# Windowed attention and a two-layer network in one program: values' parts side by side as one stationary block, and float32 transposes without copies

## The chip, the cores and the metric

The program runs on one core of a Trainium2 chip. Its time is device microseconds of one execution; three runs of the kernel before took 1107.52, 1108.76 and 1111.5 us (median 1108.76). One further look at it is a profiled execution, from which all rows below come. "Span" is the time from its first to its last instruction.

The core has a matrix engine (TensorE, PE in the profile, with its loads of stationary blocks shown as PEld), three engines for elementwise work (VectorE or DVE, ScalarE or ACT, GpSimd or POOL) and a queue that starts transfers (SP). Each takes its instructions in the order in which they stand.

## The reference

Two parts follow each other. The first is attention over 8 batches and 8 heads of 64 columns with 512 local and 32 global positions: global queries see everything, local queries see the 32 global keys and the local keys at most 32 away.

```python
s_g = scale * np.matmul(q_g, k_all.transpose(0, 1, 3, 2))
out_g = np.matmul(sm(s_g), v_all)
s_ll = scale * np.matmul(q_l, k_l.transpose(0, 1, 3, 2))
mask = np.abs(pos[:, None] - pos[None, :]) <= window
s_ll = np.where(mask, s_ll, -1000000000.0)
s_lg = scale * np.matmul(q_l, k_g.transpose(0, 1, 3, 2))
a_l = sm(np.concatenate([s_lg, s_ll], axis=-1))
out_l = np.matmul(a_l, np.concatenate([v_g, v_l], axis=2))
```

Its 8 x 544 rows of 512 columns (4352 rows) go through two layers, with weights of 512 x 2048 and 2048 x 512 that arrive as float64:

```python
h = x @ w_in
g = h * (1.0 / (1.0 + np.exp(-h)))
return (g @ w_out).astype(np.float32)
```

## The kernel before

**Parts.** To get more than the precision of the type float32r, each operand of a matmul is split into an upper part (a cast to float32r on ACT) and a lower part (the value less its upper part, on DVE or POOL). A product is three matmuls: upper by upper, upper by lower, lower by upper.

**Local attention** goes in 128 steps, 16 for a batch: a chunk c of 128 queries (4 of them) for a pair of heads (4 of them). A step has these pieces, each a function whose name begins with `st_`: load queries and keys; split them; scores on TensorE, then mask, exponential and division on DVE and ACT, into one of two buffers `probs` (lines 369 to 382); a transfer that copies `probs` into the float32r tile `rr` (line 385), since an engine that writes float32r would round; load the values, split them into `vhi` and `vlo` (lines 350 to 353); the turn: four transposes by the identity on TensorE (line 393), whose result is split into `pt_hi` on ACT and `pt_lo` on DVE (lines 396 to 398), while POOL puts beside each 32 columns of probabilities of the global queries (lines 404 to 406); and the product with the values (line 421). For each of the two heads that is three terms by two tiles of keys, with a stationary block of 128 x 64 values and 160 or 128 moving columns; in the last chunk all twelve have 160. ACT and DVE then split the product (64 rows for each head) into `xh` and `xl`, the input of the layers (lines 427 and 428), and DVE adds the 32 columns of the global queries up in `acc` (lines 433 and 435).

**Global attention** has its own pieces, named `g_`. `g_move` copies the probabilities by two transfers into float32r tiles, `g_turn` transposes them (lines 310 and 313).

**The layers** run over blocks of three or two tiles of 128 rows. A block has 16 rounds. The first layer of a round is 12 matmuls (line 550) and takes the four slices of `xh` and `xl` in turn, so the slice of the last pair of heads stands in its last three; the second layer is three matmuls for each tile (lines 569 to 571). The attention for the next block stands between them: every piece has a due time, counted in steps (`DUE`), and `fill` issues the pieces that are due after every few matmuls. The last piece of a block is therefore near its next block's start. The first block's attention stands alone at the beginning, together with the conversion of the weights, 2.6 us of DVE work for half a slice (lines 233 to 236).

TensorE's instructions stand as the program issues them. On the other engines a scheduler places them. The buffers `pt_hi` and `pt_lo` exist once, `probs` and the products' splits twice; in the banks of TensorE's results each of scores, transposes and products has one once the layers run.

Of the kernel before, what the change touches and what calls it, by code (L numbers as in the profile page):

```python
# [33 lines left out]
NEG = -8.0e9              # times the scale of 1/8: -1e9  # L34
SCALE = 0.125

# [1 line left out]
SIZES = [3, 2] + [3] * 9 + [2]       # token tiles in each block of the two layers  # L38
NLATE = 4                            # slices of the weights that take the place of the first buffers
# [19 lines left out]
PRE, PACE, LOOK = 0, 0.75, 1         # weights converted during the first steps  # L59
END = 0.6                            # how far the attention is ahead of a block  # L60
# [22 lines left out]
BUFS = dict(qk=[2, 2], raw=2, rr=1, p=2, vraw=2)  # L83
# [7 lines left out]
ND = 28  # L91

@with_exitstack
def attention_moe_kernel(ctx: ExitStack, tc: tile.TileContext, qk0_in, qk_in, v_in, gqk, wts, out):
# [7 lines left out]
    # buffers of the first steps, in two parts that later hold the last slices of the weights  # L102
# [6 lines left out]
    # until the layers start, attention has their banks too  # L109
# [33 lines left out]
    # probabilities: columns past the window stay zero  # L143
    probs = []
    for i in range(BUFS["p"]):
        t = const.tile([P, 2, 2 * P], F32, name=f"probs{i}")
        nc.gpsimd.memset(t, 0.0)
        probs.append(t)
# [239 lines left out]
    def st_turn(k, b, c, pr):  # L388
# [3 lines left out]
        for i in range(4):  # L392
            nc.tensor.transpose(t[:, i * P : (i + 1) * P].bitcast(F32R), rr[:, i * P : (i + 1) * P], ident)  # L393
# [274 lines left out]
```

## Time and profile before

| | |
|---|---|
| runs, median of three | 1108.76 us (1107.52 to 1111.5) |
| profiled execution: span | 1108.1 us |
| TensorE busy | 1042.5 us, mean granted clock 0.972 |
| DVE busy | 798.5 us |
| ACT busy | 725.1 us |
| POOL busy | 228.5 us |
| SP: copies of probabilities for local steps | 128 of 256 KB |

The profiled execution's own time beside its span is not listed; the span is 0.7 us below the median of the runs and inside their range. A row of a timeline gives start and duration in us, the engine, the line, the operation, `result<-operands`, and the shape (for a matmul stationary block, then moving columns). Matmuls overlap: the spacing of their starts says what one costs. A row of a grouped view ends with busy us and mean ns of one, then the engine's idle time just before and what ended it.

### The profile page before, as it was taken

Reading aid. Unit: us, or ns where it says so; the run is one execution under the profiler, and the core shown is the slowest. Engines: PE = TensorE matmul, PEld = TensorE weight load, DVE = VectorE, ACT = ScalarE, POOL = GpSimd, SP = SyncE. Lnnn points to the kernel's source line nnn. Section 1 sums busy time; section 2 is a strip of 40 time slices with the busy share of each in tenths; the row PEclk is TensorE's granted clock in tenths of the full one; section 3 lists DMA queues with packets and bytes.
Section 4 is the critical chain, followed back from the end, with each engine's and each line's share of the span. In section 5 each row is a group of like instructions: output and inputs, shape, how many; then the busy total and the mean of one; then the engine's idle time right before and its main releaser. Section 6 shows DMA issues by size and latency. Waiting matters only on the chain.

```text
span 1108.1 us, 21579 instructions
## 1 busy us (share of the span) xinstructions
PE 1042.5 (94%) x6824; PEld 947.8 (86%) x6824; DVE 798.5 (72%) x2467; ACT 725.1 (65%) x1933; POOL 228.5 (21%) x441
## 2 busy tenths in 40 slices
PE   5647889999999999999999999999999999999998
PEld 4646778898999999999989999999999999889996
DVE  6989998777778867766667877777777768863322
ACT  7876676776677766766567776667666658763232
POOL 8756775321100111001010111101100011100000
PEclk8678899999999999999999999999999999999999
DMA  8576554543343443342233443334333324420000
GB/s 249 179 219 188 182 170 130 156 121 117 109 145 115 138 138 110 113 148 83 82 112 112 147 130 117 111 116 158 109 109 120 111 92 148 138 76 20 1 30 19
DMA packets 74800, 134.76 MB, mean 122 GB/s; under 512 B 10432, under 2 KB 30400, under 8 KB 74688
## 3 DMA queue, kind: packets, MB, share of 16 engines
q1 hardware_dynamic: 74688, 133.40, 38.8%
q8 instruction: 54, 0.88, 0.3%
q14 instruction: 58, 0.48, 0.1%
HBM read 86.44 MB, written 8.91 MB: 86 GB/s over the span
## 4 chain that ended last, share of the span: by engine, by line
PE 80%; DVE 10%; DMA 3%; issue 3%; ACT 3%; POOL 1%; SPq 0%; DVEq 0%; ACTq 0%; POOLq 0%
PE h L550 31%; PE out L569 11%; PE out L571 10%; PE out L570 10%; PE o L421 8%; PE s L369 4%; PE t L393 3%; DVE w L234 2%; DVE w L236 1%; DMA rr<-probs 1%; DMA raw_w<-in_wts_dram 1%; DVE raw_w L233 1%; DVE pt_lo L397 1%; ACT probs L377 1%; DVE probs L373 1%
## 5 line engine op out<-in xcount | busy, mean ns | idle before, releaser
L550 PE MATMUL h<-xh,w_hi 128*128 128x384 f32 (+1 forms) x768 | 255.6, 333 | 0.1
L550 PE MATMUL h<-xh,w_lo 128*128 128x384 f32 (+1 forms) x768 | 252.3, 329 | 0.0
L550 PE MATMUL h<-xl,w_hi 128*128 128x384 f32 (+1 forms) x768 | 252.1, 328 | 0.0
L569 PE MATMUL out<-w_hi,gh 128*128 128x512 f32 x544 | 224.8, 413 | 0.0
L571 PE MATMUL out<-w_hi,gl 128*128 128x512 f32 x544 | 215.6, 396 | 3.0 <-DVE gl L560 1.8
L570 PE MATMUL out<-w_lo,gh 128*128 128x512 f32 x544 | 214.7, 395 | 0.0
L556 ACT ACTIVATE t<-h 128x384 f32<-128x384 f32 (+1 forms) x192 | 90.5, 471 | 186.2 <-PE h L550 175.8
L404 POOL CAST pt_hi<-pgt 128x64 fp32r<-128x64 f32 (+1 forms) x160 | 50.4, 327 | 726.1 <-PE o L421 719.2
L557 DVE SCALAR_TENSOR_TENSOR t<-t,h 128x384 f32<-128x384 f32 (+1 forms) x192 | 101.6, 529 | 122.7 <-ACT t L556 121.7
L550 PEld LDWEIGHTS h<-xh,w_hi 128*128 128x128 f32 x768 | 145.4, 189 | 6.0 <-ACT xh L427 0.6
L550 PEld LDWEIGHTS h<-xl,w_hi 128*128 128x128 f32 x768 | 145.5, 189 | 5.4
L550 PEld LDWEIGHTS h<-xh,w_lo 128*128 128x128 f32 x768 | 145.3, 189 | 0.0
L560 DVE TENSOR_TENSOR gl<-t,gh 128x384 fp32r<-128x384 f32 (+1 forms) x192 | 107.3, 559 | 48.5 <-PE out L571 43.1
L571 PEld LDWEIGHTS out<-w_hi,gl 128*128 128x128 f32 x544 | 102.8, 189 | 28.4 <-DVE gl L560 4.6
L377 ACT ACTIVATE probs<-probs,st 128x224 f32<-128x224 f32 x256 | 121.4, 475 | 7.3 <-DVE st L373 6.2
L373 DVE CUSTOM_DVE_ANT_0 probs<-s,mask 128x224 f32<-128x224 f32 x256 | 89.3, 384 | 50.4 <-PE s L369 47.0
L421 PE MATMUL o<-pt_hi,vhi 128*64 128x160 f32 (+1 forms) x512 | 99.4, 238 | 20.1 <-ACT pt_hi L396 7.8
L570 PEld LDWEIGHTS out<-w_lo,gh 128*128 128x128 f32 x544 | 103.6, 190 | 11.2
L569 PEld LDWEIGHTS out<-w_hi,gh 128*128 128x128 f32 x544 | 103.2, 190 | 11.4 <-ACT gh L559 0.4
L559 ACT CAST gh<-t 128x384 fp32r<-128x384 f32 (+1 forms) x192 | 94.6, 493 | 21.2 <-DVE t L557 17.8
L421 PE MATMUL o<-pt_hi,vlo 128*64 128x160 f32 (+1 forms) x512 | 96.3, 237 | 0.0
L421 PE MATMUL o<-pt_lo,vhi 128*64 128x160 f32 (+1 forms) x512 | 79.8, 238 | 16.3 <-DVE pt_lo L397 11.8
(82 smaller groups left out, 2016.5 us busy)
## 6 DMA issues: line engine op xcount, KB each, us to landing
raw<-in_qk_dram SPq DMA_DIRECT2D x100, 352.0 KB, 3.0
rr<-probs SPq DMA_DIRECT2D x128, 256.0 KB, 2.3
vraw<-in_v_dram SPq DMA_DIRECT2D x128, 128.0 KB, 2.4
raw_w<-in_wts_dram SPq DMA_DIRECT2D x28, 512.0 KB, 4.0
raw_g<-in_gqk_dram SPq DMA_DIRECT2D x32, 304.0 KB, 2.8
out_dram<-o SPq DMA_DIRECT2D x32, 256.0 KB, 2.6
raw<-in_qk_dram SPq DMA_DIRECT2D x28, 240.0 KB, 3.6
rg<-pg SPq DMA_DIRECT2D x16, 256.0 KB, 2.4
```

The costliest lines, as they stand in the source:

```text
L373: nc.vector.tensor_tensor_reduce(out=p[:, u, :W], in0=s[:, u * W : (u + 1) * W], in1=mask_of[c], scale=-SCALE, scalar=3.0e38, op0=ALU.add, ...
L377: nc.scalar.activation(p[:, u, :W], p[:, u, :W], AF.Exp, bias=st[:, u : u + 1], scale=-1.0, accum_out=st[:, 2 + u : 3 + u])
L404: nc.gpsimd.tensor_copy(out=pt_hi[:n, :, a, P:], in_=g)
L421: nc.tensor.matmul(o[:D, u * wide : u * wide + m], v[:, a, u, :], pt[:, u, a, :m], start=(i == 0), stop=(i == len(terms) - 1))
L550: nc.tensor.matmul(h[:, :nt], wt, x[:, c, :nt], start=(i == 0), stop=(i == 3 * NCC - 1))
L556: nc.scalar.activation(t[:, :nt], h[:, :nt], AF.Tanh, scale=0.5)
L557: nc.vector.scalar_tensor_tensor(out=t[:, :nt], in0=t[:, :nt], scalar=1.0, in1=h[:, :nt], op0=ALU.add, op1=ALU.mult)
L559: nc.scalar.copy(out=gh[:, :nt], in_=t[:, :nt])
L560: nc.vector.tensor_tensor(out=gl[:, :nt], in0=t[:, :nt], in1=gh[:, :nt].bitcast(F32), op=ALU.subtract)
L569: nc.tensor.matmul(o, gh[:, sl], wh, start=(f == 0), stop=False)
L570: nc.tensor.matmul(o, gh[:, sl], wl, start=False, stop=False)
L571: nc.tensor.matmul(o, gl[:, sl], wh, start=False, stop=(f == NF - 1))
```

## The change

1. **Values.** `vhi` and `vlo` become halves of one tile `vv`: for a key tile and head 64 upper columns, then 64 lower ones. The upper part of the probabilities is multiplied with all 128 columns at once, so its products with upper and lower values come out on rows 0 to 63 and 64 to 127. The lower part of the probabilities still meets the upper values alone. Four matmuls for a head instead of six.
2. **Halves.** ACT copies the lower 64 rows from TensorE's result to a new tile `xs`, DVE adds the upper 64 rows to it; so for both heads. Then ACT casts `xs` into `xh` for both heads at once (128 rows), and DVE (steps 0 to 23) or POOL (from 24, `POOLX`) subtracts it for `xl`. The sum of the global queries' columns moves from DVE to POOL, 128 rows at once.
3. **Transposes.** `probs` is the operand itself, as float32, with a float32 identity; the copies to `rr` are gone, and those of `g_move` too. In the first 12 steps there are five buffers `probs` instead of two. The check that `pg` is free waits for `g_turn`.

On TensorE, the product of step 91, the last of a block (`o91` is the result; the number after a tile's name is the step). Before:

```order
L421 MATMUL o91_9862<-pt_hi0_126,vhi91_9748 64x160
L421 MATMUL o91_9862<-pt_hi0_126,vlo91_9749 64x160
L421 MATMUL o91_9862<-pt_hi0_126,vhi91_9748 64x128
L421 MATMUL o91_9862<-pt_hi0_126,vlo91_9749 64x128
L421 MATMUL o91_9862<-pt_lo0_127,vhi91_9748 64x160
L421 MATMUL o91_9862<-pt_lo0_127,vhi91_9748 64x128
```

These six are one head's; six like them follow. With the change:

```order
L413 MATMUL o91_9358<-pt_hi0_130,vv91_9249 128x160
L415 MATMUL o91_9358<-pt_lo0_131,vv91_9249 64x160
L413 MATMUL o91_9358<-pt_hi0_130,vv91_9249 128x128
L415 MATMUL o91_9358<-pt_lo0_131,vv91_9249 64x128
L413 MATMUL o91_9358<-pt_hi0_130,vv91_9249 128x160
L415 MATMUL o91_9358<-pt_lo0_131,vv91_9249 64x160
L413 MATMUL o91_9358<-pt_hi0_130,vv91_9249 128x128
L415 MATMUL o91_9358<-pt_lo0_131,vv91_9249 64x128
```

That is both heads, in the same place between the layers' matmuls; wide and narrow ones alternate.

On ACT, from the cast or copy out of that product to the first activation of the next block (`t7_0`). Before:

```order
L427 CAST xh_7_8748<-o91_9862 64x128
L350 CAST vhi93_9978<-vraw93_9824 128x256
L559 CAST gh6_15_9856<-t6_15_9855 128x384
L342 CAST qk94_9960<-raw94_9901 128x704
L427 CAST xh_7_8748<-o91_9862 64x128
L377 ACTIVATE probs1_122,st93_9890<-probs1_122,st93_9890 128x224 x2
L381 ACTIVATE probs1_122<-probs1_122,st93_9890 128x224
L556 ACTIVATE t7_0_9925<-h7_0_9912 128x384
```

With the change:

```order
L421 COPY xs91_9367<-o91_9358 64x160
L341 CAST vv93_9469<-vraw93_9320 128x4x64
L333 CAST qk94_9451<-raw94_9392 128x704
L554 CAST gh6_15_9352<-t6_15_9351 128x384
L421 COPY xs91_9367<-o91_9358 64x160
L369 ACTIVATE probs1_120,st93_9383<-probs1_120,st93_9383 128x224 x2
L423 CAST xh_7_8296<-xs91_9367 128x128
L373 ACTIVATE probs1_120<-probs1_120,st93_9383 128x224
L551 ACTIVATE t7_0_9416<-h7_0_9403 128x384
```

The two copies stand where the two casts stood, and the cast that ends the step stands behind two exponentials.

On POOL, around the same product, with the change (before, only lines 404 and 405 stood there, turn after turn):

```order
L394 CAST pt_hi0_130<-pgt5_8145 128x2x32
L395 TENSOR_TENSOR pt_lo0_131<-pgt5_8145,pt_hi0_130 128x2x32
L430 TENSOR_TENSOR acc_134<-xs91_9367,acc_134 128x32
L424 TENSOR_TENSOR xl_7_8297<-xs91_9367,xh_7_8296 128x128
L394 CAST pt_hi0_130<-pgt5_8145 128x2x32
```

The first two rows belong to step 92; the sum and the subtraction of step 91 stand behind them.

The diff, without comments and with what only follows from it left out:

```diff
-    id32 = work.tile([P, P], F32R, tag="qk", bufs=BUFS["qk"][0], name="id32").bitcast(F32)
-    make_identity(nc, id32)
-    ident = const.tile([P, P], F32R, name="ident")
-    nc.vector.tensor_copy(out=ident, in_=id32)
+    ident = const.tile([P, P], F32, name="ident")
+    make_identity(nc, ident)
...
-    for i in range(BUFS["p"]):
-        t = const.tile([P, 2, 2 * P], F32, name=f"probs{i}")
+    for i in range(5):
+        home = const if i < BUFS["p"] else first_pool[0]
+        t = home.tile([P, 2, 2 * P], F32, name=f"probs{i}")
...
     def g_move(b, hh):
         did(("move", b, hh), ("soft", b, hh))
-        r0 = two.tile([P, 4 * P], F32R, tag="o", name=f"rg0_{b}_{hh}")
-        r1 = two.tile([P, SG], F32R, tag="rg", name=f"rg1_{b}_{hh}")
-        nc.sync.dma_start(out=r0.bitcast(F32), in_=pgs[hh][:, : 4 * P])
-        nc.sync.dma_start(out=r1.bitcast(F32), in_=pgs[hh][:, 4 * P :])
...
-            nc.tensor.transpose(tb[:, sl].bitcast(F32R), r0[:, sl], ident)
+            nc.tensor.transpose(tb[:, sl], pg[:, sl], ident)
...
-        vhi = two.tile([P, 2, 2, D], F32R, tag="vhi", name=f"vhi{k}")
-        vlo = two.tile([P, 2, 2, D], F32R, tag="vlo", name=f"vlo{k}")
+        vv = two.tile([P, 2, 2, 2, D], F32R, tag="vv", name=f"vv{k}")
+        vhi, vlo = vv[:, :, :, 0, :], vv[:, :, :, 1, :]
...
-        p = probs[k % BUFS["p"]]
+        i = k % (5 if k < RRS else BUFS["p"])
+        p, probs_of[i] = probs[i], k
...
-        rr = rr_tile(k)
-        nc.sync.dma_start(out=rr.bitcast(F32), in_=p.rearrange("p u j -> p (u j)"))
...
-            nc.tensor.transpose(t[:, i * P : (i + 1) * P].bitcast(F32R), rr[:, i * P : (i + 1) * P], ident)
+            nc.tensor.transpose(t[:, i * P : (i + 1) * P], p[:, i * P : (i + 1) * P], ident)
...
         for u in range(2):
-            terms = [(v, pt_hi, a) for a in range(2) for v in (vhi, vlo)] + [(vhi, pt_lo, a) for a in range(2)]
-            for i, (v, pt, a) in enumerate(terms):
+            for a in range(2):
                 m = wide if a == 0 or c == NC - 1 else P
-                nc.tensor.matmul(o[:D, u * wide : u * wide + m], v[:, a, u, :], pt[:, u, a, :m],
-                                 start=(i == 0), stop=(i == len(terms) - 1))
+                at = slice(u * wide, u * wide + m)
+                nc.tensor.matmul(o[:, at], vv[:, a, u].rearrange("p t d -> p (t d)"), pt_hi[:, u, a, :m],
+                                 start=(a == 0), stop=(a == 1))
+                nc.tensor.matmul(o[:D, at], vv[:, a, u, 0], pt_lo[:, u, a, :m], start=False, stop=(a == 1),
+                                 skip_group_check=(a == 1))
+        xs = two.tile([P, wide], F32, tag="xs", name=f"xs{k}")
         for u in range(2):
+            at = slice(u * wide, (u + 1) * wide)
             rows = slice(D * u, D * (u + 1))
-            src = o[:D, u * wide : u * wide + P]
-            nc.scalar.copy(out=xh[rows, pr, sl], in_=src)
-            nc.vector.tensor_tensor(out=xl[rows, pr, sl], in0=src, in1=xh[rows, pr, sl].bitcast(F32),
-                                    op=ALU.subtract)
-            gsrc = o[:D, u * wide + P : (u + 1) * wide]
-            gdst = acc[rows, pr, g0 : g0 + SG]
...
-                nc.vector.tensor_tensor(out=gdst, in0=gsrc, in1=gdst, op=ALU.add)
+            nc.scalar.copy(out=xs[rows, :], in_=o[D:, at])
+            nc.vector.tensor_tensor(out=xs[rows, :], in0=o[:D, at], in1=xs[rows, :], op=ALU.add)
+        nc.scalar.copy(out=xh[:, pr, sl], in_=xs[:, :P])
+        lows(k >= POOLX).tensor_tensor(out=xl[:, pr, sl], in0=xs[:, :P], in1=xh[:, pr, sl].bitcast(F32),
+                                       op=ALU.subtract)
+        gdst = acc[:, pr, SG * (b % 4) : SG * (b % 4 + 1)]
...
+            nc.gpsimd.tensor_tensor(out=gdst, in0=xs[:, P:], in1=gdst, op=ALU.add)
...
         if f == NF - 1:
-            while ("rg", 0) in state or ("rg", 1) in state:
-                advance(stream[done][0])
```

More of the change, by code (lines that the diff above doesn't have):

```diff
@@ L82 @@
 HEADS = (7, 2)
-BUFS = dict(qk=[2, 2], raw=2, rr=1, p=2, vraw=2)
+BUFS = dict(qk=[2, 2], raw=2, p=2, vraw=2)
 PTS = 0
@@ L91 @@
 ND = 28
+POOLX = 24
 @with_exitstack
@@ L186, in qk_tiles @@
                 pool.tile([P, SKV], F32R, tag="klo", bufs=bufs[1], name=f"klo{name}"))
-    def rr_tile(k):
-        if k % 2 and k < RRS and first[0]:
-            held[0].add(f"rr{k}")
-            return first_pool[0].tile([P, 4 * P], F32R, tag="rr", bufs=1, name=f"rr{k}")
-        return work.tile([P, 4 * P], F32R, tag="rr", bufs=BUFS["rr"], name=f"rr{k}")
     def lows(pool):
@@ L260, in g_scores @@
         hi, lo = state.pop(("gqk", p))
-        did(("scores", b, p), *([("move", b - 1, p // 2)] if b else []))
+        did(("scores", b, p), *([("turn", b - 1, p // 2)] if b else []))
         free(f"_g{b}_{p}")
@@ L352, in st_vsplit @@
             out=vlo, in0=vraw, in1=vhi.bitcast(F32), op=ALU.subtract)
-        tiles["v", k] = vhi, vlo
+        tiles["v", k] = vv
     def st_scores(k, b, c, pr):
@@ L411, in st_out @@
         sl = slice(i * P, (i + 1) * P)
-        vhi, vlo = tiles.pop(("v", k))
+        vv = tiles.pop(("v", k))
         pt_hi, pt_lo = pt_tiles(k)
```

21 lines of the change are left out of this document (11 added, 10 removed).

## Prediction

> **What bounds the kernel now.** I read the page's busy shares first, then the busy times by stretch, then the waits of single lines. Busy shares and slices say where one engine is full:
>
> ```profile
> PE 1042.5 (94%) x6824; PEld 947.8 (86%) x6824; DVE 798.5 (72%) x2467; ACT 725.1 (65%) x1933; POOL 228.5 (21%) x441
> ...
> PE   5647889999999999999999999999999999999998
> ...
> DVE  6989998777778867766667877777777768863322
> ```
>
> The stretches (columns: length, then busy us of PE, PEld, DVE, ACT, POOL, with the granted clock, DMA share and GB/s last):
>
> ```profile
> 27.70:85.00 57.30, 32.87 (x241) 29.69 (x241) 51.25 (x153) 44.32 (x124) 37.97 (x50) 0.71 0.64 198
> ...
> 133.00:166.00 33.00, 28.39 (x179) 25.07 (x178) 32.37 (x71) 24.45 (x63) 24.87 (x26) 0.93 0.55 171
> ...
> 742.00:832.00 90.00, 89.98 (x602) 82.41 (x602) 67.52 (x223) 62.43 (x170) 10.23 (x32) 1.00 0.39 124
> ...
> 916.00:983.00 67.00, 65.69 (x528) 60.29 (x528) 57.44 (x209) 52.36 (x154) 9.63 (x24) 1.00 0.42 132
> ```
>
> There are two regimes. Up to about 206 us DVE decides: 51.25 of 57.30 us (89%) and 32.37 of 33.00 (98%), because it converts the weights beside the attention. After that TensorE is never idle (89.98 of 90 us) at full clock, while DVE has 25% and ACT 31% to spare. So in the second regime a microsecond off TensorE's own stream is a microsecond off the end, and a microsecond on DVE, ACT or POOL is free until it makes TensorE wait. In the first regime it is the other way round.
>
> **What the change does to TensorE.** The values' product, in start times (a matmul's own duration overlaps its successor, so I take start to start):
>
> ```profile
> 508.49 0.24 PE L421 MATMUL o<-pt_hi,vhi 128*64 128x160 f32 x1
> ...
> 509.38 0.43 PE L569 MATMUL out<-w_hi,gh 128*128 128x512 f32 x1
> ```
> ```profile
> 528.77 0.23 PE L421 MATMUL o<-pt_hi,vhi 128*64 128x160 f32 x1
> ...
> 529.57 0.45 PE L569 MATMUL out<-w_hi,gh 128*128 128x512 f32 x1
> ```
> ```profile
> 503.50 0.47 PE L393 MATMUL t<-ident,rr 128*128 128x128 f32 x4
> 503.81 0.46 PE L569 MATMUL out<-w_hi,gh 128*128 128x512 f32 x1
> ```
>
> A step of the last chunk has twelve matmuls of 160 columns in 0.89 us, 0.074 each. Any other step has six of 160 and six of 128 in 0.80, so a column costs 0.09/192 = 0.00047 us and a matmul of 128 columns 0.059. Now eight remain. Four have a stationary block of 128 columns instead of 64. Four float32r transposes, with 128 stationary and 128 moving columns, take 0.31, 0.077 each: 0.018 more than 0.059. If that surcharge falls on the four wide matmuls, a usual step costs 2 x 0.092 + 2 x 0.077 + 2 x 0.074 + 2 x 0.059 = 0.60 and saves 0.20, a last-chunk step 4 x 0.092 + 4 x 0.074 = 0.66 and saves 0.23. Without it they save 0.27 and 0.30. After 206 us lie 104 of the 128 steps (76 usual, 28 last-chunk): 22 to 29 us. I take **25**, nearer the surcharge, as its row is the only one with 128 and 128 columns.
>
> The Trainium skill, "TensorE: Matmul & The Clock Gate", section LDWEIGHTS, speaks against the change: a load takes its columns / 1.2 ns, so 107 ns for 128 columns; by it the wide matmuls would cost 0.107 each, a usual step would save 0.11 and the kernel some 11 us. The trace disagrees: its transposes load 128 columns every 77 ns.
>
> **Transposes from float32.** Their number, shape and places stay; only operand types change, and the copies go. Nothing in the trace runs a plain float32 matmul. Lower bound zero: the same 128 columns stream once. Upper bound: the array takes such an operand in four passes, each with a load of its own, 3 x 0.077 = 0.23 more per transpose. After 206 us there are 104 x 4 + 6 batches x 10 = 476 of them: 0 to 110 us. I take **0**, because the float32r transpose already moves all 32 bits in one go: line 397 subtracts the rounded part from the transposed value to get the lower part, and there would be nothing left if the array had rounded.
>
> **The copies removed.**
>
> ```profile
> L385 SPq DMA_DIRECT2D rr<-probs x128: 464/471/862, 17.7 to 1018.3; - x128
> ...
>   DVE probs L373: 2.4, 3
>   PE t L393: 1.7, 4
> ...
> DMA to landing us min/median/max: 2.2/2.3/4.7
> ```
>
> A copy lasts 2.3 us, but TensorE waited only 1.7 us for all 128, and DVE 2.4. The order of TensorE leaves room for the landing, so in the steady part they are worth under 2 us, **1** say. That the probabilities now stay occupied until the transpose costs nothing there: the transpose of step k stands on TensorE before the scores of step k+2, which need the buffer.
>
> **What moves between engines.**
>
> ```profile
> L428 DVE TENSOR_TENSOR xl<-o,xh 64x128 fp32r<-64x128 f32 x256 | 71.9, 281 | 23.7 <-ACT xh L427 19.8
> ...
> L427 ACT CAST xh<-o 64x128 fp32r<-64x128 f32 x256 | 65.6, 256 | 44.6 <-PE o L421 32.6 <-DVE acc L435 5.0 <-DVE acc L433 1.9
> ...
> L351 POOL TENSOR_TENSOR vlo<-vraw,vhi 128x256 fp32r<-128x256 f32 x28 | 25.8, 920 | 4.1 <-ACT vhi L350 4.0
> ...
> L435 DVE TENSOR_TENSOR acc<-o,acc 64x32 f32<-64x32 f32 x192 | 33.4, 174 | 0.0
> ...
> L405 POOL TENSOR_TENSOR pt_lo<-pgt,pt_hi 128x64 fp32r<-128x64 f32 x128 | 45.9, 359 | 7.0
> ```
>
> Per step DVE gives up 2 x 281 + 2 x 174 = 910 ns and takes two adds of 64x160, 281 plus 32 columns at (281 - 174)/96 = 1.1 ns, about 315 each: 280 ns less. ACT gives up 2 x 256 and takes two copies of 64x160 (about 285 each) and one cast of 128x128 (about 260): 320 ns more. POOL takes a 128x32 sum (about 250, under the 359) and, from step 24, a 128x128 subtraction (between 359 and 920, say 500). In the stretch 916 to 983, the tightest, ACT rises from 52.4 to 56.2 of some 64 us, 88%: covered, though it is now the fullest engine behind TensorE; I allow 1 us. POOL goes from some 11% to 21%: covered. In its queue the sum and subtraction of step k stand behind the pt_hi and pt_lo pieces of step k+1, so what TensorE needs next is not queued behind them.
>
> **What is late next** is the way from the values' product to the layers. Before: ACT, DVE, done. Now: ACT copy, DVE add, ACT copy, DVE add, ACT cast, POOL subtraction, one after the other. It matters at the start of a block, where the last step's slice is used by the last three of twelve matmuls:
>
> ```profile
> 829.39 0.32 PE L369 MATMUL s<-qk 128*128 128x224 f32 x1
> ...
> 831.27 0.26 ACT L427 CAST xh<-o 64x128 fp32r<-64x128 f32 x1
> ...
> 832.04 0.47 ACT L377 ACTIVATE probs<-probs,st 128x224 f32<-128x224 f32 x1
> ...
> 832.41 0.19 ACT L377 ACTIVATION_READ_ACCUMULATOR probs<-probs,st 128x1 f32 x1
> ...
> 833.74 0.33 PE L550 MATMUL h<-xl,w_hi 128*128 128x384 f32 x1
> ```
>
> The product ends at 829.39 and the lower part is needed at 833.74, 4.35 us later. With the new order, the second ACT copy ends at 831.27 + 0.28, its add at about 831.9, the cast stands behind two exponentials that end at 832.60 and is done at about 832.9, POOL's subtraction at about 833.5: in time by 0.2 us. The least margin is that of the last block but one:
>
> ```profile
> 981.52 0.45 PE L569 MATMUL out<-w_hi,gh 128*128 128x512 f32 x1
> ...
> 985.08 0.33 PE L550 MATMUL h<-xl,w_hi 128*128 128x384 f32 x1
> ```
>
> 3.56 us. Read in the same way, seven of the eleven block starts after the first have less than 5 us, the other four more than 6. I allow each of the seven 0 to 1.4 us and take **3** for all (0 to 10).
>
> **The first 206 us.**
>
> ```profile
> 17.65 4.25 DMA rr<-probs
> ...
> 57.47 7.73 DMA raw_w<-in_wts_dram
> ```
> ```profile
> L234 DVE SCALAR_TENSOR_TENSOR w<-w,raw_w x36: 424/693/1777, 18.6 to 199.5; 128x512 uint32<-128x512 uint32 x28, 128x256 uint32<-128x256 uint32 x8
> ```
> ```profile
> L234 DVE SCALAR_TENSOR_TENSOR w<-w,raw_w 128x512 uint32<-128x512 uint32 x28 | 30.3, 1083 | 0.6
> ```
> ```profile
> L428 DVE TENSOR_TENSOR xl<-o,xh x256: 259/283/289, 30.3 to 1047.6; 64x128 fp32r<-64x128 f32 x128
> ```
>
> The chain of waits ran through a copy at 17.65, which goes (five probability buffers instead of two free the next scores as well), and through a weight load of 7.73 us whose way gets clearer: up to 8 us of gain. Against it: until step 23 DVE subtracts from an SBUF copy instead of from PSUM. Line 234, with both inputs in SBUF, ranges from 424 to 1777 ns beside a busy POOL, line 428, reading PSUM, only from 259 to 289. Line 234's mean of 1083 (30.3 us over 28) lies 0.39 us over its median, which on some 20 steps is 8 us of DVE, full there. Its own work is otherwise equal, 2 x 315 + 280 against 910 ns. I take **+1** (-8 to +8).
>
> **The sum.** 1108.1 - 25 - 1 + 1 + 3 + 1 = 1087 us against the profiled span; the median of the runs, 1108.8, is 0.7 higher, so the forecast is **1088 us**. Its own range takes products of 22 to 29, block starts of 0 to 10 and the first part at -8 to +8, not all at one end: 1077 to 1102.
>
> **Rivals.**
>
> *The array takes a float32 transpose in several passes* (slower than before). For it: the trace has no such matmul, and a copy per step was made only to change the operand's type. Against it: the bit-keeping float32r transpose at 0.077. The price is per transpose, on TensorE, in the part where nothing hides it. Two passes at 0.060 (128 columns) to 0.077: 476 x 0.060 to 0.077 = 29 to 37 us, so 1116 to 1125. Four passes: three more streams of 128 columns, 476 x 0.18 = 86, up to 110 with their loads, so 1174 to 1198. It decides from 22/476 = 0.046 us more per transpose: beyond that the change loses. Chances 0.10 and 0.15.
>
> The Trainium skill holds both sides: "FP8 and Floating Point Precision", TensorE Precision Notes, says that true float32 makes four passes through the array; "TensorE: Matmul & The Clock Gate", Terms, calls the transpose mode four times faster for float32, which would undo them. No run here shows which holds for this form; by the first the time is the 1174 or more above, by the second the forecast.
>
> *The longer way to the layers decides.* If the cast on ACT, at 88% in the stretch from 916, and POOL's subtraction come 2.5 us late at the seven block starts and the twelve close steps lose 0.4 us each, 17.5 + 4.8 us are lost instead of 4: 1088 + 18 = 1106, no change. For it: six links through three queues instead of three through two. Against: the hand-made case above still has 0.2 us. Chance 0.09.
>
> *The first part gets short.* Without the copies DVE finds its work early and the 8 us are gained in full: 1088 - 9 = 1079. Against: 98% busy, and the SBUF reads. Chance 0.07.
>
> **How the numbers follow.** The forecast gets 0.59. The range of **1074 to 1122** holds its own, the short first part, the rival of no change and most of the two-pass one; left out is above all the four-pass case. About 0.3% (3.3 us) is what a measurement of this kernel can tell from no change. Faster by more: nearly all of 0.59, 0.07 and a little of the third case, 0.67. Within: most of that case, 0.07. Slower: the multi-pass cases and a rest, 0.26.
>
> **What would show it.** The product of a usual step from start to next matmul 0.53 to 0.60 us, with 0.80 before; the four transposes 0.31 again (0.55 or 1.0 if there are passes); TensorE idle at block starts, with ACT's cast or POOL's subtraction named as releaser, 0 to 1.4 us each; DVE some 28 us less busy after 206 us and ACT some 33 more; DVE's 128x128 subtraction of the first steps above 0.3 us in the mean; the first block's end near 206. I am wrong if the transposes' matmuls last longer than before, if TensorE idles more than 10 us after 206, or if the wide matmuls are spaced by 0.107.

## The result and the profile after

The changed kernel takes 1115.23 us (median of 4 runs, 1114.42 to 1115.69), the kernel before 1108.39 us beside it. The ratio is 1.0055 with a 95% interval of 1.0039 to 1.007: slower, where 1088 us had been forecast. The profiled execution of the changed kernel spans 1113.9 us, 5.8 us more than the one before.

The page of the changed kernel: busy shares, then TensorE's and VectorE's slices.

```profile
PE 1044.4 (94%) x6312; PEld 954.2 (86%) x6312; DVE 797.8 (72%) x2234; ACT 772.1 (69%) x2061; POOL 328.5 (29%) x676
...
PE   5467779899999999999999999999999999999998
...
DVE  6988998768777877776667777777777667873322
```

TensorE has 512 matmuls fewer and yet is as busy as before (1042.5 us then). Over the first seven slices together it is a little less busy than before (5467779 against 5647889, in tenths). The same four stretches as in the prediction say where (length, then busy us of PE, PEld, DVE, ACT, POOL; granted clock, DMA share and GB/s last):

```profile
27.70:85.00 57.30, 32.21 (x172) 28.87 (x172) 51.23 (x128) 43.05 (x116) 39.51 (x57) 0.62 0.45 140
133.00:166.00 33.00, 23.51 (x128) 20.85 (x128) 30.73 (x60) 22.27 (x55) 22.26 (x24) 0.84 0.40 128
...
742.00:832.00 90.00, 89.76 (x558) 82.69 (x557) 66.75 (x201) 66.50 (x182) 20.85 (x57) 1.00 0.27 83
916.00:983.00 67.00, 67.00 (x489) 62.03 (x488) 55.61 (x182) 56.76 (x165) 18.10 (x48) 1.00 0.30 94
```

The two regimes are as they were. In the late stretches TensorE is full, and ACT in the tight one stands at 56.8 us, close to the 56.2 worked out. In the first regime VectorE is as busy as before from 27.7 to 85 us (51.23 against 51.25), but with 128 instructions done instead of 153, and TensorE did 172 matmuls instead of 241. Part of both differences is the change itself, which takes four matmuls and one VectorE instruction out of a step; the rest is work that comes later.

The line between the regimes is the start of the second block, the first row of the layers' first matmul there. Before, and with the change:

```profile
206.58 0.34 PE L550 MATMUL h<-xh,w_hi 128*128 128x384 f32 x1
```
```profile
220.18 0.35 PE L545 MATMUL h<-xh,w_hi 128*128 128x384 f32 x1
```

So **13.6 us were lost before the second block**: 7.7 before the first (its first matmul starts at 94.1 instead of 86.4 us), 5.9 between the two. From the second to the start of the last block (1055.13 and 1061.37) the change **gained 7.4 us**, 841.2 instead of 848.6, and the last block 0.47 more: 13.61 - 7.37 - 0.47 = 5.77.

The 7.4 us can be split up, since TensorE's starts follow each other there almost without a gap (4.2 us idle before, 2.5 with the change). I added up the spacings of all starts in that part by the tile that the matmul writes:

| TensorE, second to last block, us | before | change |
|---|---|---|
| products with the values | 86.9 | 70.9 |
| transposes of the steps | 30.7 | 37.2 |
| global transposes | 4.7 | 5.7 |
| global scores | 17.5 | 18.7 |
| local scores | 46.3 | 46.3 |
| layers | 662.4 | 662.4 |

Minus 16.0 for the products, plus 6.5 for the transposes, plus 2.2 for the global parts. The products and transposes of a usual step with the change:

```profile
541.13 0.23 PE L413 MATMUL o<-pt_hi,vv 128*128 128x160 f32 x1
541.21 0.23 PE L415 MATMUL o<-pt_lo,vv 128*64 128x160 f32 x1
...
541.79 0.44 PE L564 MATMUL out<-w_hi,gh 128*128 128x512 f32 x1
...
545.99 0.60 PE L383 MATMUL t<-ident,probs 128*128 128x128 f32 x4
546.34 0.48 PE L564 MATMUL out<-w_hi,gh 128*128 128x512 f32 x1
```

The product takes 0.66 us where 0.53 to 0.60 was forecast, four transposes 0.35 instead of 0.29 to 0.31. What TensorE waited for from the second block's start to the last's (us in total, times, longest):

```profile
PE gt L301 <- DVE xs L422: 1.3, 5, 0.4
PE h L545 <- ACT xh L423: 0.7, 1, 0.7
PE o L415 <- DVE st L372: 0.5, 1, 0.5
```

The block starts cost 0.7 us in all. The six links from the product to the layers are not the trouble.

### The profile page after: what moved, and what is told of

Same layout as the page of the kernel before. It is cut to its first block, busy times and chain, and to the rows that moved or that the text cites. A ratio compares the mean times of both kernels' runs of the same rounds, so it can differ in the third digit from the quotient of the medians.

```text
span 1113.9 us, 20011 instructions
## 1 busy us (share of the span) xinstructions
PE 1044.4 (94%) x6312; PEld 954.2 (86%) x6312; DVE 797.8 (72%) x2234; ACT 772.1 (69%) x2061; POOL 328.5 (29%) x676
## 4 chain that ended last, share of the span: by engine, by line
PE 82%; DVE 10%; ACT 4%; issue 2%; DMA 2%; POOL 0%; SPq 0%; ACTq 0%; DVEq 0%; POOLq 0%
PE h L545 32%; PE out L564 11%; PE out L566 10%; PE out L565 10%; PE s L360 5%; PE t L383 4%; PE o L413 4%; PE o L415 3%; DVE w L230 2%; DVE w L232 1%; DVE raw_w L229 1%; DMA raw_w<-in_wts_dram 1%; DVE gl L555 1%; DVE pt_lo L387 1%; DMA raw_g<-in_gqk_dram 1%
## 5 line engine op out<-in xcount | busy, mean ns | idle before, releaser
L415 PE MATMUL o<-pt_lo,vv 128*64 128x160 f32 (+1 forms) x512 | 103.3, 241 | 27.4 <-DVE pt_lo L387 26.3
L413 PE MATMUL o<-pt_hi,vv 128*128 128x160 f32 (+1 forms) x512 | 107.3, 275 | 12.6 <-ACT pt_hi L386 5.4
L413 PEld LDWEIGHTS o<-pt_hi,vv 128*128 128x128 f32 x512 | 99.8, 199 | 18.8 <-issue 9.0
```

What stands on the lines that cost most here:

```text
L413: nc.tensor.matmul(o[:, at], vv[:, a, u].rearrange("p t d -> p (t d)"), pt_hi[:, u, a, :m], start=(a == 0), stop=(a == 1))
L415: nc.tensor.matmul(o[:D, at], vv[:, a, u, 0], pt_lo[:, u, a, :m], start=False, stop=(a == 1), skip_group_check=(a == 1))
```

## Experiments

"Second block" is the start of its first matmul in the profiled run, the same place as the two rows above, and "first block" that of the block before it. "Steady part" is from the second to the last block's start. Each such start is from one execution, while the times are medians. All ratios are to the kernel before on the same chip.

### The values alone

```diff
 (kernel before, with the values' product and its way out of the change)
-        xs = two.tile([P, wide], F32, tag="xs", name=f"xs{k}")
+        xs = two.tile([P, wide], F32, tag="xs", bufs=1, name=f"xs{k}")
-BUFS = dict(qk=[2, 2], raw=2, rr=1, p=2, vraw=2)
+BUFS = dict(qk=[2, 2], raw=2, rr=1, p=2, vraw=1)
```

> Kernel before with the values' part of the change alone: copies and float32r transposes stay as they were. To make room, the tile for the summed halves and the raw values have one buffer each instead of two. The changed kernel's second block starts 13.6 us later than before (220.18 against 206.58 us), and the rest of its span is 7.8 us shorter. Theory H: the 13.6 us are lost by the values' halves (VectorE 27.1 us for sums and subtractions in the first part instead of 20.8, and a longer chain). Then the second block starts at 216 to 222 us here, the twelve products become eight in 0.66 us instead of 0.80, the transposes stay at 0.29, 104 steps save 14.6 us, and the time is 1104 to 1109 us. Rival T: they are lost by the transposes without copies (the probabilities stay occupied until TensorE has turned them). Then the second block starts at 204 to 209 us and the time is 1092 to 1097 us.

Measured: 1115.49 us, ratio 1.0058 (1.0036 to 1.0079). Second block at 222.6, product 0.66, transposes 0.29, steady part 839.4. The place of theory H, but later than it said, and the time is 6 us above its range. The steady part gained 9.2 us rather than 14.6 or more: the second block of this run lasts 96.1 us against 93.8 before, and the last but one 72.7 against 71.8. Its single buffers are a change of their own, so this run says only that the product costs 0.66 with either transpose. (Its first block starts at 98.4 us; a run below looks at the buffer.)

### The transposes alone, and with their copies

```diff
 (changed kernel, with the old values)
-        vv = two.tile([P, 2, 2, 2, D], F32R, tag="vv", name=f"vv{k}")
+        vhi = two.tile([P, 2, 2, D], F32R, tag="vhi", name=f"vhi{k}")
+        vlo = two.tile([P, 2, 2, D], F32R, tag="vlo", name=f"vlo{k}")
```

> Changed kernel with the old values (two blocks of 64 columns, twelve matmuls, upper and lower parts straight from TensorE's result): only the float32 transposes without copies are left of the change. Theory H: the second block starts at 204 to 209 us as before, four transposes take 0.35 us instead of 0.295, which over 104 steps and the global ones is 6 to 7 us; time 1113 to 1117 us. Rival T: the second block starts at 216 to 222 us and the time is 1125 to 1131 us.

Measured: 1120.27 us, ratio 1.0102 (1.0081 to 1.0123). Four transposes 0.35, steady part 854.3, 5.7 more than before. The second block starts at 212.5: between the two theories, so neither holds. To part the type from the missing copies:

```diff
 (kernel before)
-    ident = const.tile([P, P], F32R, name="ident")
-    nc.vector.tensor_copy(out=ident, in_=id32)
+    ident = const.tile([P, P], F32, name="ident")
+    make_identity(nc, ident)
-            nc.tensor.transpose(t[:, i * P : (i + 1) * P].bitcast(F32R), rr[:, i * P : (i + 1) * P], ident)
+            nc.tensor.transpose(t[:, i * P : (i + 1) * P], rr[:, i * P : (i + 1) * P], ident)
```

> Kernel before, with its two probability buffers and its copies kept (now into float32 tiles); only the transposes and the identity are float32. The kernel with all of the change but the values starts its second block at 212.5 us, 5.9 later than before. Theory P: the float32 transposes themselves lose this (0.71 us for four in the first part, where before has 0.29 to 0.49). Then the second block starts at 210 to 215 us here too, four transposes take 0.35 later on, and the time is 1116 to 1122 us. Rival O: it is the missing copies (other order on the engines, the probabilities occupied until the turn). Then the second block starts at 205 to 209 us and the time is 1112 to 1116 us.

Measured: 1121.15 us, ratio 1.0102 (1.0082 to 1.0121); second block at 210.3, steady part 856.8. By place and time that is theory P. But the first block starts at 86.3 us, as before (86.4), although its transposes take 0.71; the 3.7 us are all lost between the first and the second block, where four take 0.35. Twelve steps at 0.06 are 0.7 us. So theory P named the place and not the reason; VectorE's order is another one here than in the kernel before, which the fills below take up. Taking the copies away is worth 856.8 - 854.3 = 2.5 us in the steady part, little more than the 2.1 by which it differs between two orders of one kernel below (835.4 and 833.4).

### The halves only from step 24 on

```diff
 (changed kernel)
+        if k < 24:
+            (the old product and its way out, with vhi and vlo as halves of vv)
+            return
```

> Changed kernel, but steps 0 to 23 use the old twelve matmuls and the old way out of TensorE's result; from step 24 all is as in the changed kernel. Theory H: the second block starts at 204 to 210 us and the time is 1100 to 1105 us, faster than both kernels. Rival T: the second block starts at 216 to 222 us, and the time stays at 1112 to 1118 us.

Measured: 1105.74 us, ratio 0.9966 (0.9951 to 0.9981). Second block at 212.7, steady part 840.2. Some 7.5 us of the 13.6 went with the halves, 6 us stayed, as with the transposes alone. Between the theories again.

### The lower part on GpSimd in all steps

```diff
 (changed kernel)
-POOLX = 24
+POOLX = 0
```

> Changed kernel with the subtraction for the lower part on GpSimd in all steps, not only from step 24. It takes 12.7 us (23 of 551 ns) off VectorE before the second block. Theory H in its form that VectorE's busy time is what is lost: second block 5 to 12 us earlier (208 to 215 us), time 1103 to 1110 us. If it is the longer chain instead, or GpSimd's queue is the bound there (67% busy before the second block), the second block starts at 218 to 228 us, and the time is 1113 to 1123 us.

Measured: 1111.86 us, ratio 1.0029 (1.0015 to 1.0042); second block at 215.6, 0.6 us beyond what was expected of VectorE's busy time, and 1.9 us above the range of times. Another queue bound (the 218 or later) did not come. The order on VectorE is another one than in the changed kernel, so the 4.6 us gained are not a price of the subtraction alone.

### What a product and a transpose cost

```diff
 (changed kernel; few = the first 16 columns)
+                if k >= 24 and k % 2 == 0:
+                    nc.tensor.matmul(o[:, few], vv[:, a, u].rearrange("p t d -> p (t d)"), pt_hi[:, u, a, :16], ...)
+                if k >= 24 and k % 2 == 1:
+                    nc.tensor.matmul(o[:D, few], vv[:, a, u, 0], pt_lo[:, u, a, :16], ...)
-        for i in range(4):
+        for i in [j for j in range(4) for _ in range(2 if k >= 24 and k % 4 >= 2 else 1)]:
```

> Changed kernel; from step 24 on even steps have four more wide matmuls (128 stationary columns) and odd steps four more narrow ones (64), each with only 16 moving columns, and two steps of four turn each block twice. The first 16 columns of every chunk are so counted twice: the result is another one. Theory L (the product is bound by loading the stationary blocks: 0.66 us for 768 loaded columns, 0.00086 us each): the product takes 0.66 + 4 x 0.110 = 1.10 us in even steps and 0.66 + 4 x 0.055 = 0.88 in odd ones. Theory S (bound by the moving columns, 0.00047 us each): 0.69 in both. Theory F (0.077 for a block of 128, as a float32r transpose of before): 0.97 in even steps. Eight float32 transposes take 0.70 us if each costs 0.0875, and 0.65 if the surplus of 0.06 over float32r is paid once at the change of type.

One execution, 1168.5 us. A double turn and an even step of that run:

```profile
608.74 1.03 PE L383 MATMUL t<-ident,probs 128*128 128x128 f32 x8
609.53 0.37 PE L264 MATMUL gs<-qk_g 128*64 128x272 f32 x1
...
612.42 0.23 PE L413 MATMUL o<-pt_hi,vv 128*128 128x160 f32 x1
612.49 0.21 PE L417 MATMUL o<-pt_hi,vv 128*128 128x16 f32 x1
...
613.50 0.39 PE L552 MATMUL h<-xh,w_hi 128*128 128x384 f32 x1
```

Over the usual steps the product takes 1.074 us in even ones and 0.899 in odd ones. A stationary block of 128 columns costs (1.074 - 0.660) / 4 = 0.104 us with only 16 moving columns, one of 64 costs 0.060 (0.097 and 0.060 in last-chunk steps). That is nearest to theory L: the product is bound by loading, and 768 stationary columns are loaded for a step before and after the change. The Trainium skill, "TensorE: Matmul & The Clock Gate", section LDWEIGHTS, gives columns / 1.2 ns, by estimate 0.107 and 0.053 us; the runs agree nearly on the wide one and are a little above on the narrow. Eight float32 transposes take 0.79, each further one (0.79 - 0.35) / 4 = 0.11. That is more than either expectation (0.70 and 0.65). Inside the group the starts lie 0.108 us apart, and the matmul behind it starts 0.03 us after the last transpose: so four take 0.35 and not 4 x 0.11, and a price read from one group of four is too low. The same for the old transposes:

```diff
 (kernel before)
-        for i in range(4):
+        for i in [j for j in range(4) for _ in range(2 if k >= 24 and k % 4 >= 2 else 1)]:
```

> Kernel before; from step 24 on two steps of four turn each block twice, by float32r transposes, with the same result. With float32 the second four cost 0.44 us (0.35 to 0.79), 0.11 each, as much as loading 128 columns cost in the product (0.105). Theory L (the forecast's 0.077 for a float32r transpose, 0.31 over four, was a reading at the edge of a group, and a float32r one is bound by the same load): eight take 0.29 + 0.44 = 0.73 us. Theory F (a float32r transpose really loads and streams 128 columns in 0.074 to 0.077): eight take 0.59 to 0.61 us.

```profile
620.76 0.80 PE L393 MATMUL t<-ident,rr 128*128 128x128 f32 x8
621.40 0.41 PE L550 MATMUL h<-xh,w_hi 128*128 128x384 f32 x1
```

One execution, 1123.6 us. Eight take 0.64, in all double turns 0.63 to 0.65: between the theories. A further float32r transpose costs (0.64 - 0.29) / 4 = 0.086 us. So 0.077 was too low, and a float32 one costs some 0.02 more than a float32r one. But 0.086 is also less than the 0.104 of a wide matmul of the product, with the same 128 stationary columns: theory L does not hold for float32r transposes. (Both float32 and float32r rows stand in the trace as f32.)

### Copies kept, halves from step 24 on

```diff
 (kernel before, values of the change from step 24 on; xs and vraw with one buffer each)
+WIDE0 = 24
```

> Kernel before with its copies and float32r transposes, and the values' part of the change from step 24 on only (one buffer for the summed halves and for the raw values, to make room). Theory: the loss of the first part comes from the halves and from the float32 transposes, and both are gone: second block at 205 to 209 us; from there to the last block's start 834 to 841 us (838 to 840 if the single buffers stall the second block as in the run with the values alone); time 1092 to 1101 us, faster than both kernels. Rival: the single buffer for the raw values is what made the first part of the run with the values alone 16 us longer; then the second block starts at 213 us or later and the time is 1101 to 1108 us.

Measured: 1101.63 us, ratio 0.9924 (0.9903 to 0.9945). Steady part 835.2, as expected, but the second block at 213.2: the rival, the first block alone starts 7.7 us later (94.1 instead of 86.4). With a second buffer for the raw values while the memory of the first steps is there:

```diff
+        if k % 2 and k < RRS and first[0]:
+            held[0].add(f"vraw{k}")
+            vraw = first_pool[0].tile([P, 2, 2, D], F32, tag="vraw", bufs=1, name=f"vraw{k}")
+        else:
             vraw = raws.tile([P, 2, 2, D], F32, tag="vraw", bufs=BUFS["vraw"], name=f"vraw{k}")
```

> Kernel before with copies and float32r transposes, and the values' part of the change from step 24 on; the raw values have a second buffer in the memory of the first steps until step 11, so the first block is as before. Theory (the 7.7 us that the first block lost in the run with one buffer come from that buffer): first block starts at 85 to 88 us, second at 204 to 208, from there to the last block's start 834 to 837 us; time 1092 to 1098 us, faster than both kernels. Rival (the order on the engines shifts by the narrower memory anyway): second block at 210 us or later, time 1099 us or more.

Measured: 1095.36 us, ratio 0.9867 (0.9851 to 0.9884). First block at 84.2, second at 208.4, steady part 835.4. The theory's range of time holds, its place of the second block is missed by 0.4 us (that execution took 1098.17 us, 2.8 above the median). VectorE's order is that of the kernel before, while with one buffer it was another, so buffer and order are not told apart. It beats both kernels by more than 1%.

### Another order, from fills that nobody reads

In the first part VectorE, ACT, POOL and SP stand in an order that a scheduler chose, and an edit there may move it. Two fills that nobody reads test what an order is worth (each also holds one of the four buffers `st` for a moment):

```diff
 (kernel before)
+        if k in (1, 2):
+            spare = small.tile([P, 8], F32, tag="st", name=f"spare{k}")
+            nc.gpsimd.memset(spare, 0.0)
```

> Kernel before with two fills of 128 x 8 elements on GpSimd, that nobody reads, in steps 1 and 2. They cost some 0.2 us of GpSimd, but the scheduler then orders the first part anew: of the first 470 instructions of VectorE some 140 stand elsewhere, as many as with the float32 transposes. Theory R (the 3.6 us that the float32 transposes with copies lost in the first part are a new order and not the transposes): the second block starts 2 to 6 us from 206.6, to one side or the other, and the time differs from the kernel before by 2 to 6 us. Rival Q (the order does not matter, the transposes' own time does): second block at 205.6 to 207.6 us, time within 1.5 us of before.

Measured: 1115.62 us, ratio 1.0053 (1.0034 to 1.0071), as much as the whole change. Theory R holds:

```profile
213.32 0.39 PE L553 MATMUL h<-xh,w_hi 128*128 128x384 f32 x1
```

The second block starts 6.7 us later, and the steady part (848.1) is what it was. VectorE shows where the time went: up to the second block it is busy 187.4 us instead of 180.3, with 478 instructions instead of 476, and idle as long as before (25.9 and 26.3 us). Two lines took most of it; before, then with the fills:

```profile
L382 DVE TENSOR_SCALAR probs<-probs,st 128x224 f32<-128x224 f32 x21 | 11.6, 553 | 0.1
...
L379 DVE TENSOR_SCALAR st<-st 128x2 f32<-128x2 f32 x26 | 7.2, 275 | 2.1 <-ACT probs L377 1.8
```
```profile
L382 DVE TENSOR_SCALAR probs<-probs,st 128x224 f32<-128x224 f32 x22 | 15.1, 688 | 0.2
...
L379 DVE TENSOR_SCALAR st<-st 128x2 f32<-128x2 f32 x26 | 13.1, 502 | 2.7 <-ACT probs L377 2.5
```

What makes the same instructions longer in this order was not tried. With the fills on VectorE in steps 13 and 14:

> Kernel before with two such fills on VectorE in steps 13 and 14: some 15 of VectorE's first 470 instructions and 11 of ScalarE's stand elsewhere. Theory R: a smaller shift of the second block, 0 to 3 us to one side or the other. Rival Q: second block at 205.6 to 207.6 us, time within 1.5 us of before.

Measured: 1108.3 us, ratio 0.9979 (0.9966 to 0.9993); second block at 205.6, 1.0 us earlier. That fits both theory R and rival Q, and decides nothing by itself.

> Changed kernel with one fill of 128 x 8 elements on GpSimd in step 0 that nobody reads; some 145 of VectorE's first 440 instructions then stand elsewhere. Theory H (the 13.6 us are the halves' and the transposes' own): second block at 217 to 223 us, time 1112 to 1118 us. Rival R (a good part is the order that the scheduler happened to choose; in the kernel before two fills moved the second block by 6.7 us): second block at 208 to 215 us, time 1103 to 1110 us, or as far to the other side.

Measured: 1109.88 us, ratio 1.0012 (1.0 to 1.0024). One fill in step 0 of the changed kernel (the same lines with `k in (0,)`) made it 5 us faster, and rival R holds:

```profile
212.77 0.34 PE L548 MATMUL h<-xh,w_hi 128*128 128x384 f32 x1
```

Here VectorE is busy longer than in the changed kernel's own order (190.8 us up to the second block, 187.1 there) and idle less (22.0 and 33.1 us): this order saves idle time and not work. Of the 7.4 us, 6.9 are gained before the first block (87.2 instead of 94.1).

Fills on the version with copies and halves from step 24:

> Copies and float32r transposes kept, halves from step 24 on, raw values with a second buffer in the first steps (1095 us), with one fill on GpSimd in step 0: some 140 of VectorE's first 470 instructions stand elsewhere, as with the two fills in the kernel before. Theory R: the second block moves from 208.4 us by 2 to 7 us, most likely to later (212 to 215, time 1099 to 1103 us), as in the kernel before. Rival Q (its order is not sensitive): within 1.5 us of 1095.

Measured: 1100.18 us, ratio 0.9924 (0.9908 to 0.9939); second block at 212.4, 4.0 later, as theory R said (the medians differ by 4.8).

> The same version with two fills on VectorE in steps 13 and 14, which made the kernel before 1.2 us faster (second block 1.0 us earlier). Theory R: second block at 205 to 210 us, time 1092 to 1097 us.

Measured: 1094.5 us, ratio 0.9873 (0.9856 to 0.9889), the fastest, together with the 1095.36 of the version without the fills. The time is as theory R said, the second block 1.0 us earlier than it said:

```profile
204.03 0.34 PE L586 MATMUL h<-xh,w_hi 128*128 128x384 f32 x1
```

The starts of the second block side by side. In a row of this table VectorE's instructions up to that block stand in the same order, as the traces show:

| order of VectorE | second block, us |
|---|---|
| kernel before | 206.6; float32r turns doubled from step 24 204.6; copies, halves from step 24 208.4 |
| two fills on GpSimd | 213.3; copies, halves from step 24, one fill 212.4 |
| two fills on VectorE | 205.6; copies, halves from step 24, the same fills 204.0 |
| changed kernel | 220.2; the run with extra matmuls 218.6 |
| changed kernel, one fill | 212.8 |
| only the transposes of the change | 212.5; changed kernel, halves from step 24 212.7 |
| float32 transposes with copies | 210.3 |

The double turn and the extra matmuls change nothing before step 24, and all engines stand as in the kernel that they were made from: 206.6 and 204.6, 220.2 and 218.6 say that one execution differs from another by some 2 us. Within a row the largest difference is 3.8. So the moves by fills on GpSimd (6.7 and 7.4 us, for fills that last 0.10 us each) go with the order and not with the scatter of executions, and those by fills on VectorE are too small to tell.

From the first to the second block all seven runs with float32 transposes take 124.0 to 126.6 us, the nine with float32r 118.8 to 127.2, five of them under 121; that the transposes have a share there is not excluded.

## Why the prediction was wrong

**What bounds the kernel** was read rightly: TensorE's own stream after the second block's start, and before it something else, with VectorE fullest.

**The step that failed is "The first 206 us".** It was put at +1 with bounds of -8 to +8, and measured +13.6. It turned the sign: with +1 in its place the terms measured below add up to -6.8 us, a faster kernel. Its two sides were a clearer way for the transfers and VectorE's reads beside a busy POOL. The first did not show: without the copies the second block starts at 212.5, with them at 210.3, both with float32 transposes. The second side was right in kind. VectorE's groups of the changed kernel up to 217 us, about when the second block's last product is done:

```profile
L422 DVE TENSOR_TENSOR xs<-o,xs 64x160 f32<-64x160 f32 x46 | 14.4, 313 | 3.2 <-ACT xs L421 2.3
...
L424 DVE TENSOR_TENSOR xl<-xs,xh 128x128 fp32r<-128x128 f32 x23 | 12.7, 551 | 0.0
```

27.1 us for sums and subtractions, where lines 428, 433 and 435 of before have 12.8 + 2.8 + 5.2 = 20.8 up to 201 us: 6.3 us more, with 8 allowed. What the prediction did not have is the order. An edit in the first steps may arrange the first part anew, and among three orders of the kernel before the second block moved by 7.7 us (205.6 to 213.3), about as much as either bound of the term. Of the 13.6 us, 7.4 went with one fill that does nothing. What is left, 6.2 us, is about VectorE's extra work, but with two orders of the changed kernel and three of the kernel before, whose starts overlap (212.8 and 213.3), how much of the loss is the change's own **stays open**. TensorE's granted clock in this part is lower with the change (0.62 against 0.71 from 27.7 to 85 us). That alone is not the cause: the kernel before with two fills on GpSimd has 0.60 there and with double turns 0.65, and their first blocks start at 86.1 and 84.0 us, no later than its own.

**The product** was the right mechanism with the wrong size: 25 us forecast, 22 to 29 in its range, 16.0 measured. The term mis-sized is the price of a wide matmul, 0.077 to 0.092 taken and 0.104 measured with 16 moving columns. I had taken the 0.077 from groups of four transposes and used it against the 107 ns that the Trainium skill gives in "TensorE: Matmul & The Clock Gate", section LDWEIGHTS. Both halves of that step fail: in a row such a transpose costs 0.086, and a transpose is no stand-in for a wide matmul of the product. The page's figure is nearly right for the product and too high for the transposes. By it the usual step saves 0.11, the last-chunk step 0.17 and the kernel 13 us (the prediction put 0.11 on every step and had 11), which is too little by 3, while mine is too much by 9.

A step loads 768 stationary columns before and after; what falls is its moving columns, 1728 to 1152 in a usual step. By the prediction's 0.00047 us a column these are 0.81 and 0.54 us, an estimate, and by the prices of further matmuls the loads of the change are 4 x 0.104 + 4 x 0.060 = 0.66. The step took 0.80 and takes 0.66: before, the moving columns set the time, and now the loads do, so part of the saving is lost to them. The forecast went by the first bound and a surcharge, not by the second.

**The transposes from float32** were taken at 0 (0 to 110) and cost 6.5 us in the steps and 1.0 in the global part, 0.11 us each in a row instead of 0.086. The 1.15 us of the global scores go with them: these take 18.6 to 18.7 us in every run with float32 transposes and 17.5 in every run with float32r ones; why, no run shows. It is not one of the rivals' prices: two passes would have been 29 to 37 us, four 86 or more. The Trainium skill's four passes for true float32 ("FP8 and Floating Point Precision", TensorE Precision Notes) do not show in a transpose here.

**The copies** were put at 1 us; the run that has them beside float32 transposes puts them at 2.5, with the caveat above. **The way to the layers** was put at 3 us (0 to 10) and cost 0.7: the hand-made case with 0.2 us to spare was good enough, and the rival of the longer way is out. **ACT and POOL** stayed covered.

**VectorE after 206 us.** 28 us less were forecast, 604.1 and 596.6 measured, from the second block's start to the last's:

```profile
206.60:1055.10 848.50, 844.30 (x5587) 772.83 (x5586) 604.13 (x1958) 557.40 (x1494) 92.43 (x268) 1.00 0.36 112
```
```profile
220.20:1061.40 841.20, 838.70 (x5172) 771.50 (x5171) 596.56 (x1759) 595.39 (x1605) 182.26 (x478) 1.00 0.26 77
```

The durations of its instructions there add up to 692.5 and 670.4, 22 less; these sums exceed the busy time, so records overlap, and it fell by less. ACT rose by 38 with 33 forecast.

**The sum by its terms**: -16.00 (products) - 0.47 (the last block) + 6.49 and 1.02 (transposes) + 1.15 (global scores, not in the sum at all) - 0.02 (the rest) + 13.61 (the first part) = +5.8 us, where -21 was forecast. Of the signs of being wrong that were named beforehand two came, longer transposes and wide matmuls near 0.107; the third did not, as TensorE idled 2.5 us.

## What to carry to other kernels

A part that a scheduler may order anew after an edit has a scatter of its own: measure it with an edit that does nothing before a few microseconds there are put down to a change, and make the bounds of a prediction at least as wide. Take the price of a short matmul from repeating that very matmul in place, not from a short group of another kind. And a change that pays where one engine is full is best made there alone: with the old values in the first 24 steps and the copies kept, the same idea gives 1.3% instead of losing 0.55%.

## What the hardware showed that was not expected

**VectorE waited out a GpSimd instruction to its end.** The subtraction of line 424 reads both inputs from SBUF. One of them in the changed kernel's first part, with what POOL did:

```profile
40.99 1.27 DVE L424 TENSOR_TENSOR xl<-xs,xh 128x128 fp32r<-128x128 f32 x1
```
```profile
40.41 1.71 POOL L235 TENSOR_TENSOR w_lo<-w,w_hi 128x512 fp32r<-128x512 f32 x1
```
```profile
117.76 0.27 DVE L424 TENSOR_TENSOR xl<-xs,xh 128x128 fp32r<-128x128 f32 x1
```

At 117.76, after POOL's instruction had ended, it takes 0.27 us; at 40.99 it ends 0.14 us after POOL's (42.26 and 42.12). Of the 24 on VectorE nine take more than 0.5 us, and each of the nine ends 0.14 to 0.16 us after a subtraction on POOL does. It is not slowed in proportion but held:

```profile
L424 DVE TENSOR_TENSOR xl<-xs,xh x24: 269/305/1368, 35.3 to 222.6; 128x128 fp32r<-128x128 f32 x24
```

The mean of 551 ns is thus a mixture of 0.28 us and of what was left of POOL's instruction, and depends on the order. Instructions with one input in TensorE's results are not held: line 428 before stays at 261 to 286 ns, though 38 of the 48 up to the second block meet an instruction on POOL, and so do the sums of the changed kernel:

```profile
L422 DVE TENSOR_TENSOR xs<-o,xs x46: 295/317/319, 31.5 to 210.8; 64x160 f32<-64x160 f32 x46
```

The Trainium skill, "SBUF — State Buffer", section "SBUF: two separate sides", says so of a VectorE instruction with two SBUF inputs beside GpSimd: the pair of ports is an exclusive lock for the whole instruction. These rows agree. How much of an order's gain or loss comes from such meetings was not shown: with the fills on GpSimd the kernel before lost as much as VectorE's instructions grew, while the changed kernel's fill saved idle time.
